# One wide product for the last queries of two heads, and a clamp and a rounding that change engines

## The chip, the core and the metric

The kernel runs on one core of a Trainium2 chip. The metric is the device time of one execution in microseconds (us). Of the core's engines this text uses short names: PE is TensorE (products; PEld its weight loads, which are rows of their own), DVE is VectorE, ACT is ScalarE, POOL is GpSimd, SP is SyncE, which issues most DMAs. Each engine works through its own list of instructions in order, and waits at an instruction until the semaphores that it names have come.

## The reference

Three stages in float32: an attention with a block-causal mask, a feed-forward layer that takes the maximum of three products, and a layer of four experts whose outputs are summed with weights.

```python
# attention: q, k, v of shape (4, 8, 576, 64)
scores = np.matmul(q, k.transpose(0, 1, 3, 2)) / np.sqrt(64)
scores = np.where(block_i >= block_j, scores, -1000000000.0)   # blocks of 64 positions
attn = softmax(scores)                                         # with + 1e-09 below the line
x = np.matmul(attn, v).transpose(0, 2, 1, 3).reshape(2304, 512)
# first layer: w1, w2, w3 (512, 768), w_out (768, 512)
x = np.maximum(np.maximum(x @ w1, x @ w2), x @ w3) @ w_out
# experts: w1 (4, 512, 1024), w2 (4, 1024, 512), p = domain_probs / (row sum + 1e-09)
out = sum(p[:, e:e + 1] * (np.maximum(x @ w1[e], 0) @ w2[e]) for e in range(4))
```

## The kernel before

**Numbers in two words.** A product in full float32 takes several passes on PE. Most products here are made from two rounded words instead: a number x is split into a high word (x rounded to the type float32r) and a low word (x minus the high word), and a product of two such numbers takes the products high by high, high by low and low by high. The heads of the first batch (`g < H`, eight of 32) use plain float32 in attention; the other 24 use split words.

**Attention.** The heads are walked in pairs. A pair's heads share one tile of queries: the last 64 of each head's 576 queries stand together in the tile `p4`, 128 rows, 64 of one head and 64 of the other. `scores` (lines 225 to 284) makes the scores of a tile of queries, takes the row extremes on DVE, the exponentials on ACT with their row sums, and lets POOL divide the rows by the sums (line 282). `turn_probs` (line 299) turns the tiles by PE transposes into a PSUM tile `tt`, from where ACT copies the high word `eh` (line 319) and DVE subtracts to get the low word `el` (line 320). Part 2 of it is the shared tile of last queries, turned once per pair: its columns are key block by key block, and within a block first the 64 queries of one head, then the 64 of the other.

`values` (line 357) makes the product with v for a split head. The stationary operand `vs[:, h, j]` holds the high word of v in columns 0 to 63 and the low word in 64 to 127, for one block j of keys, so that one product gives both in the upper and lower 64 rows of the result `pv`. What streams past is `eh` and then, in products of its own, `el`; both are summed into the same columns of PSUM. For the shared tile `products` (line 324) takes the head's 64 columns of each of the five key blocks, five products of 64 columns with `eh` and five with `el`, into columns 384 to 447. In the end ACT copies the other 64 rows to `tmp` (line 385) and DVE adds them to the head's own (line 386), which gives the head's part of `xf`, the transposed x of the pair. `moe1_inputs` (line 519) splits `xf` into `xh` (ACT, line 528) and `xl` (DVE, line 529) when a batch's heads are through.

**First layer.** `moe1` makes the first layer for one batch. Its products (`m`, line 510, 288 columns) are mixed by a planner into the attention of the next batch: `Filler` takes so many units after each step of a head, ten units behind. For the first batch the weights come from `Convert`, for the other three from a copy in HBM that it wrote. ACT and DVE evict the products (lines 546 and 548), POOL splits the hidden values (lines 550 and 551).

**Conversion.** The weights of the first layer are read as raw words of 64 bits, two words of 32 each, in 26 pieces, 18 of 512 columns and 8 of 384, and put together again as float32 values. `first` takes the magnitude of the upper word (ACT, line 433) and the scaled lower word (ACT, line 435). `second` clamps the magnitude (line 440), shifts it (442), joins it with the sign (443), and adds the lower word (POOL, 447). `third` rounds it to the high word (line 456, by the helper at line 82) and subtracts for the low word (457). `tick` runs these three as a pipeline, one or two pieces apart. The magnitudes have two buffers, the lower words one.

```python
nc.vector.tensor_scalar(a, a, MOST, LEAST, op0=ALU.min, op1=ALU.max)   # L440, the clamp
rounded(nc.gpsimd, high, a)                                            # L456, the rounding (runs at L82)
```

**Experts.** The last stage (lines 645 to 915) is products with split words throughout.

**Order.** The program is scheduled when it is built: a scheduler with a model of the engines' times puts the instructions of the first two stages into order on each engine. A small edit can so move many instructions against each other.

## Time and profile before

| | us |
|---|---|
| median of three runs | 1324.93 (1322.38 to 1325.15) |
| profiled execution, its own time | 1325.09 |
| its span, first to last instruction | 1323.4 |
| PE busy, PEld busy | 1286.8, 1185.8 |
| DVE, ACT, POOL busy | 917.8, 541.2, 629.9 |
| mean granted TensorE clock | 0.991 |

A busy time is a union: weight loads overlap each other and the products, and products overlap too, so a product's own length (say 256 ns) is not the time that it adds. That is read from the start of one load to the start of the next. A group's row ends with the idle time of its engine just before it and what ended it. The order rows below have no times: they show how the instructions stand in an engine's list, and in brackets the engines (with a number that says nothing here) whose semaphores an instruction waits for.

### The profile page before, as it was taken

The page shows a single profiled execution, that of the slowest core. Times are in us where ns is not written, and L with a number is a line of the kernel's source. Part 1 is how long each engine was busy: PE and PEld are TensorE (multiplying, and loading weights), DVE is VectorE, ACT ScalarE, POOL GpSimd, SP SyncE. Part 2 cuts the span into 40 slices and gives each one's busy share as a digit, 9 for nine tenths or more (in the row PEclk, how much of TensorE's full clock was granted, in tenths as well). Part 3 has the DMA queues.
Part 4 walks back from the last instruction along what each step waited for, and adds up shares of the span by engine and source line. Part 5 has one row for each costly group of instructions (what it writes and reads, how often), then busy time and mean ns, then how long its engine had stood idle before and what let it go on. Part 6 is the DMA issues. An engine that isn't in the chain of part 4 may idle for free.

```text
span 1323.4 us, 20932 instructions
## 1 busy us (share of the span) xinstructions
PE 1286.8 (97%) x7670; PEld 1185.8 (90%) x7670; DVE 917.8 (69%) x1685; ACT 541.2 (41%) x1219; POOL 629.9 (48%) x639
## 2 busy tenths in 40 slices
PE   7899999999999999999999999999999999999998
PEld 5669889999999989988999998999999899999997
DVE  6878999555656562178767788777777876777753
ACT  5676666444544430143333343333333433333331
POOL 4965776333334342165444455444444644454420
PEclk9899999999999999999999999999999999999999
DMA  8746677555444355232222223222222133222211
GB/s 204 216 122 167 200 224 204 162 156 133 141 123 116 112 176 161 79 96 64 76 69 64 64 64 95 81 64 64 74 79 72 55 110 91 64 64 64 64 33 48
DMA packets 146982, 142.85 MB, mean 108 GB/s; under 512 B 64576, under 2 KB 112704, under 8 KB 146880
## 3 DMA queue, kind: packets, MB, share of 16 engines
q1 hardware_dynamic: 144480, 132.18, 34.0%
q10 hardware_dynamic: 2400, 9.34, 3.1%
q8 instruction: 60, 0.98, 0.3%
q14 instruction: 42, 0.34, 0.1%
HBM read 114.86 MB, written 17.30 MB: 100 GB/s over the span
## 4 chain that ended last, share of the span: by engine, by line
PE 79%; DVE 8%; issue 3%; DMA 3%; POOL 3%; ACT 2%; SPq 0%; ACTq 0%; POOLq 0%; DVEq 0%
PE m L796 24%; PE m L510 17%; PE o L861 10%; PE o L859 10%; PE o L860 10%; PE st L250 3%; PE pv L374 2%; PE tt L314 2%; DMA q<-q 1%; PE pv L345 1%; POOL p L282 1%; ACT p L271 1%; DVE arena L443 1%; DVE t L718 1%; DMA pr<-in_moe_domain_probs 1%
## 5 line engine op out<-in xcount | busy, mean ns | idle before, releaser
L510 PE MATMUL m<-xh,wt 128*128 128x288 f32 x1152 | 258.0, 302 | 6.5 <-DVE mt L548 5.5
L859 PE MATMUL o<-w2h,hh 128*128 128x512 f32 x576 | 225.4, 392 | 4.9 <-DVE arena L866 4.9
L861 PE MATMUL o<-w2h,hl 128*128 128x512 f32 x576 | 225.5, 392 | 1.3 <-DVE hl L824 1.3
L860 PE MATMUL o<-w2l,hh 128*128 128x512 f32 x576 | 225.2, 391 | 0.0
L510 PEld LDWEIGHTS m<-xh,wt 128*128 128x128 f32 x1152 | 191.4, 188 | 9.1 <-DVE mt L548 5.3
L824 DVE SCALAR_TENSOR_TENSOR hl<-c,hh 128x384 fp32r<-128x384 f32 x144 | 168.3, 1189 | 37.4 <-ACT hh L823 37.1
L689 POOL TENSOR_TENSOR w2l<-r,w2h 128x512 fp32r<-128x512 f32 x96 | 130.1, 1375 | 89.8 <-ACT w2h L688 89.8
L510 PE MATMUL m<-xl,wt 128*128 128x288 f32 x576 | 170.2, 295 | 0.0
L689 POOL TENSOR_TENSOR sl<-s,sh 128x1024 fp32r<-128x1024 f32 x48 | 116.6, 2429 | 77.5 <-ACT sh L688 77.5
L689 POOL TENSOR_TENSOR al<-r,ah 128x512 fp32r<-128x512 f32 x48 | 64.7, 1348 | 180.6 <-ACT ah L688 177.2
L866 DVE SCALAR_TENSOR_TENSOR arena<-o,pr,arena 128x512 f32<-128x512 f32 x126 | 93.6, 743 | 71.5 <-PE o L861 71.4
L859 PEld LDWEIGHTS o<-w2h,hh 128*128 128x128 f32 x576 | 108.6, 189 | 24.0 <-DVE arena L866 6.0
L861 PEld LDWEIGHTS o<-w2h,hl 128*128 128x128 f32 x576 | 108.5, 188 | 22.5 <-DVE hl L824 1.7
L823 ACT ACTIVATE hh<-c 128x384 fp32r<-128x384 f32 x144 | 71.0, 519 | 135.9 <-DVE c L818 135.9
L860 PEld LDWEIGHTS o<-w2l,hh 128*128 128x128 f32 x576 | 108.6, 189 | 17.8
L282 POOL TENSOR_SCALAR p<-p,sm 128x128 f32<-128x128 f32 (+2 forms) x144 | 89.4, 640 | 58.7 <-DVE sm L280 27.9
L510 PEld LDWEIGHTS m<-xl,wt 128*128 128x128 f32 x576 | 108.4, 188 | 0.7
L271 ACT ACTIVATE p<-st,mn 128x128 f32<-128x128 f32 (+3 forms) x144 | 78.7, 553 | 51.1 <-DVE mn L264 50.9
L688 ACT CAST ah<-r 128x512 fp32r<-128x512 f32 x48 | 29.8, 620 | 156.3 <-issue 124.2
L548 DVE TENSOR_TENSOR mt<-m,mt 128x288 f32<-128x288 f32 x96 | 43.5, 454 | 63.8 <-PE m L510 61.5
L510 PE MATMUL m<-hh,wo 128*128 128x288 f32 x384 | 84.5, 301 | 0.4 <-ACT arena L559 0.4
L688 ACT CAST w2h<-r 128x512 fp32r<-128x512 f32 x96 | 59.1, 619 | 44.3 <-PE o L861 35.0
(166 smaller groups left out, 3000.1 us busy)
## 6 DMA issues: line engine op xcount, KB each, us to landing
wt<-held SPq DMA_DIRECT2D x54, 512.0 KB, 4.0
r<-in_moe_w SPq DMA_DIRECT2D x48, 512.0 KB, 3.9
r<-in_moe_w SPq DMA_DIRECT2D x96, 256.0 KB, 2.7
arena<-in_moe_w SPq DMA_DIRECT2D x18, 512.0 KB, 4.5
held<-wt SPq DMA_DIRECT2D x18, 512.0 KB, 3.4
wo<-held SPq DMA_DIRECT2D x12, 768.0 KB, 4.3
q<-q ACTq DMA_DIRECT2D x26, 304.0 KB, 4.5
arena<-in_q SPq DMA_DIRECT2D x32, 144.0 KB, 3.3
```

The lines of the kernel that those rows point to most:

```text
L271: nc.scalar.activation(x, st[:, o:o + w], ACTF.Exp, bias=mn[:, col:col + 1], scale=-1.0, accum_out=sm[:, col:col + 1],)
L282: nc.gpsimd.tensor_scalar(x, x, sm[:, col:col + 1], 1.0, op0=ALU.mult, op1=ALU.mult)
L510: nc.tensor.matmul(out=out_, lhsT=w, rhs=x, start=m == 0, stop=m == n - 1)
L688: nc.scalar.copy(dst_h, raw)
L689: (low or nc.gpsimd).tensor_tensor(dst_l, raw, f(dst_h), op=ALU.subtract)
L796: ins = nc.tensor.matmul(out=m, lhsT=w, rhs=x, start=start and n == 0, stop=stop and n == 3 * KH - 1, skip_group_check=True,)
L823: nc.scalar.activation(h, src, ACTF.Relu)
L824: nc.vector.scalar_tensor_tensor(l, src, 0.0, f(h), op0=ALU.max, op1=ALU.subtract)
L859: nc.tensor.matmul(out=o, lhsT=hh[:, ts], rhs=wh, start=i == 0, stop=False)
L860: nc.tensor.matmul(out=o, lhsT=hh[:, ts], rhs=wl, start=False, stop=False)
L861: nc.tensor.matmul(out=o, lhsT=hl[:, ts], rhs=wh, start=False, stop=i == G - 1)
L866: nc.vector.scalar_tensor_tensor(acc, ov, pr[:, tt, e:e + 1], acc, op0=ALU.mult, op1=ALU.add)
```

## The change

Two things are put together.

The shared tile gets one tile `e4` for both words, laid out as key block, head, word, query. For one head and one key block, the 64 columns of the high word and the 64 of the low word now lie side by side, and one product of 128 columns takes both. Its result fills columns 384 to 511 of `pv`: high-word products in 384 to 447, low-word products in 448 to 511. They are no longer summed in PSUM, so the copy to `tmp` takes 512 columns, DVE adds the last 64 columns into a new tile `last` (after's line 408), and once per pair POOL adds `last` to the last 64 columns of `xf` (after's line 410). Heads of the first batch use the high word of `e4` alone, in products of 64 columns as before.

In the conversion the clamp goes from DVE to POOL (after's line 462), and the rounding from POOL to ACT (it runs at line 80 of the helper).

```diff
--- before.py
+++ after.py
@@ -300,10 +300,15 @@
 
         hd = heads[g]
         banks = PARTS[part]
-        w = (1024, 256, 640)[part]
-        eh = ap_.tile([P, w], F32 if g < H else F32R, name="eh", tag=f"eh{part}", bufs=1)
-        el = None if g < H else ap_.tile([P, w], F32R, name="el", tag=f"el{part}", bufs=1)
-        (pairs[g // 2] if part == 2 else hd)["e", part] = (eh, el)
+        if part == 2:
+
+            e4 = ap_.tile([P, 5, 2, 2, 64], F32R, name="e4", tag="e4", bufs=1)
+            pairs[g // 2]["e4"] = e4
+        else:
+            w = (1024, 256)[part]
+            eh = ap_.tile([P, w], F32 if g < H else F32R, name="eh", tag=f"eh{part}", bufs=1)
+            el = None if g < H else ap_.tile([P, w], F32R, name="el", tag=f"el{part}", bufs=1)
+            hd["e", part] = (eh, el)
         pt = hd["p"] + [pairs[g // 2]["p4"]]
         for n in banks:
             o = 512 * (n - banks[0])
@@ -313,6 +318,16 @@
                 k0 = S - P if j == 4 else j * P
                 nc.tensor.transpose(tt[:, c:c + P], pt[i][:, k0:k0 + P], ident)
                 c += P
+            if part == 2:
+                j0, j1 = BANKS[n][0][0], BANKS[n][-1][0] + 1
+                high, low = (e4[:, j0:j1, :, x] for x in range(2))
+                src = tt[:, 0:c].rearrange("x (j h q) -> x j h q", h=2, q=64)
+                if g < H:
+                    nc.scalar.copy(f(high), src)
+                    continue
+                nc.scalar.copy(high, src)
+                nc.vector.tensor_tensor(low, src, f(high), op=ALU.subtract)
+                continue
             if g < H:
                 (nc.scalar.copy if n else nc.vector.tensor_copy)(eh[:, o:o + c], tt[:, 0:c])
                 continue
@@ -321,15 +336,12 @@
         if part == 1 and g % 2 == 0:
             turn_probs(g, 2)
 
-    def products(g, part):
-
-        h = g % 2
+    def products(part):
+
         todo = []
         for j in KEYS[part]:
             q0 = max(P, P * j)
-            todo.append((j, slice(q0 - P, 384), part, slice(BASE[j] + q0 - 512 * 2 * part, BASE[j] + 512 - 512 * 2 * part)))
-        if part:
-            todo += [(j, slice(384, 448), 2, slice(j * P + h * 64, j * P + h * 64 + 64)) for j in range(5)]
+            todo.append((j, slice(q0 - P, 384), slice(BASE[j] + q0 - 512 * 2 * part, BASE[j] + 512 - 512 * 2 * part)))
         return todo
 
     def values32(g, part):
@@ -339,11 +351,15 @@
             hd["pv"] = [ps_v.tile([P, 512], F32, name=f"pv{i}", tag="v") for i in range(2)]
             et = hd["e", 0][0]
             nc.tensor.matmul(out=hd["pv"][0][lo, 0:P], lhsT=vraw[:, h, 0], rhs=et[:, 0:P], start=True, stop=True)
-        for n, (j, to, which, of) in enumerate(products(g, part)):
-            et = (pairs[g // 2] if which == 2 else hd)["e", which][0]
-            rows = hi if j == 4 else both
+        et = hd["e", part][0]
+        todo = [(j, both, to, et[:, of]) for j, to, of in products(part)]
+        if part:
+            for j in range(5):
+                rows = hi if j == 4 else both
+                todo.append((j, rows, slice(384, 448), f(pairs[g // 2]["e4"][rows, j, h, 0])))
+        for n, (j, rows, to, x) in enumerate(todo):
             nc.tensor.matmul(
-                out=hd["pv"][1][lo, to], lhsT=vraw[rows, h, j], rhs=et[rows, of],
+                out=hd["pv"][1][lo, to], lhsT=vraw[rows, h, j], rhs=x,
                 start=part == 0 and n == 0, stop=j == 4,
             )
         if part == 0 and h == 0:
@@ -367,25 +383,31 @@
                     out=hd["pv"][0][:, 0:P], lhsT=vs[:, h, 0], rhs=et[:, 0:P], start=n == 0, stop=n == 1
                 )
         pv = hd["pv"][1]
-        todo = products(g, part)
-        for n in range(2):
-            for m, (j, to, which, of) in enumerate(todo):
-                et = (pairs[g // 2] if which == 2 else hd)["e", which][n]
-                nc.tensor.matmul(
-                    out=pv[:, to], lhsT=vs[:, h, j], rhs=et[:, of],
-                    start=part == 0 and n == 0 and m == 0, stop=part == 1 and n == 1 and j == 4,
-                )
+        todo = [(j, to, et[:, of]) for et in hd["e", part] for j, to, of in products(part)]
+        if part:
+            todo += [(j, slice(384, 512), pairs[g // 2]["e4"][:, j, h]) for j in range(5)]
+        for n, (j, to, x) in enumerate(todo):
+            nc.tensor.matmul(out=pv[:, to], lhsT=vs[:, h, j], rhs=x, start=part == 0 and n == 0, stop=j == 4)
         if part == 0 and h == 0:
             pairs[g // 2]["xf"] = mp.tile([P, S], F32, name="xf", tag="xf", bufs=4)
         xf = pairs[g // 2]["xf"]
         own, other = (lo, hi) if h == 0 else (hi, lo)
         qs = (slice(0, P), slice(P, S))[part]
-        src = hd["pv"][part][:, 0:qs.stop - qs.start]
-        tmp = ap_.tile([P, S - P], F32, name="tmp", tag="tmp", bufs=1)[own, 0:qs.stop - qs.start]
+        w = qs.stop - qs.start
+        n = (P, 512)[part]
+        src = hd["pv"][part][:, 0:n]
+        tmp = ap_.tile([P, 512], F32, name="tmp", tag="tmp", bufs=1)[own, 0:n]
         nc.scalar.copy(tmp, src[other])
-        nc.vector.tensor_tensor(xf[own, qs], src[own], tmp, op=ALU.add)
+        nc.vector.tensor_tensor(xf[own, qs], src[own, 0:w], tmp[:, 0:w], op=ALU.add)
         if part == 0:
             return
+
+        if h == 0:
+            pairs[g // 2]["last"] = ap_.tile([P, 64], F32, name="last", tag="last", bufs=1)
+        last = pairs[g // 2]["last"]
+        nc.vector.tensor_tensor(last[own], src[own, w:n], tmp[:, w:n], op=ALU.add)
+        if h:
+            nc.gpsimd.tensor_tensor(xf[:, S - 64:S], xf[:, S - 64:S], last, op=ALU.add)
         del heads[g]
 
 
@@ -437,7 +459,7 @@
         def second(self, i):
             a = self.buf(i, "a")
             au, high = a.bitcast(U32), self.words(i)[1]
-            nc.vector.tensor_scalar(a, a, MOST, LEAST, op0=ALU.min, op1=ALU.max)
+            nc.gpsimd.tensor_scalar(a, a, MOST, LEAST, op0=ALU.min, op1=ALU.max)
 
             nc.vector.tensor_scalar(au, au, 3, None, op0=ALU.logical_shift_left)
             nc.vector.scalar_tensor_tensor(
@@ -453,7 +475,7 @@
                 tag, bufs = ("wt", WT) if n < 3 * NF else ("wo", 2)
                 self.made[n] = mp.tile([P, 2, tiles[n].shape[1], P], F32R, name=tag, tag=tag, bufs=bufs)
             high, low = (self.made[n][:, j, s].rearrange("p a f -> p (a f)") for j in range(2))
-            rounded(nc.gpsimd, high, a)
+            rounded(nc.scalar, high, a)
             nc.vector.tensor_tensor(low, a, f(high), op=ALU.subtract)
             nc.sync.dma_start(
                 out=held[n][:, :, s.start * P:s.stop * P],
```

On PE, the shared tile's products of the thirteenth split head (the results are `pv_4044` before and `pv_4001` after, the stationary operand is `vs`, what streams is `eh` and `el`; `m` is the first layer), before:

```order
L510 MATMUL m<-xh,wt 128x288
L374 MATMUL pv_4044<-eh,vs 128x256
L374 MATMUL pv_4044<-eh,vs 128x64 x5
L374 MATMUL pv_4044<-el,vs 128x256
L374 MATMUL pv_4044<-el,vs 128x64 x5
L510 MATMUL m<-xh,wt 128x288
```

and after:

```order
L532 MATMUL m<-xh,wt 128x288
L390 MATMUL pv_4001<-eh,vs 128x256
L390 MATMUL pv_4001<-el,vs 128x256
L390 MATMUL pv_4001<-e_3972,vs 128x128 x5
L532 MATMUL m<-xh,wt 128x288
```

Ten products of 64 columns have become five of 128, behind the 256-column products of the third key block, and nothing else stands between.

On DVE, the conversion beside the fifth split head (`arena` holds a piece's words, `wt` the finished weights; line 440 is the clamp, 442 the shift, 443 the joining, 457 the low word), before:

```order
L320 TENSOR_TENSOR el<-tt,eh 128x128 [waits Activation_49]
L440 TENSOR_SCALAR arena<-arena 128x512 [waits Activation_49]
L457 TENSOR_TENSOR wt<-arena,wt 128x512 [waits DMAHW2_49,Pool_49]
L442 TENSOR_SCALAR arena<-arena 128x512 [waits DVE_49]
L386 TENSOR_TENSOR xf<-pv_2156,tmp 64x128 [waits Activation_49]
L443 SCALAR_TENSOR_TENSOR arena<-arena 128x512 [waits DMAHW7_49,DVE_49]
L440 TENSOR_SCALAR arena<-arena 128x512 [waits Activation_49]
```

and after, where the shift is line 464, the joining 465, the low word 479:

```order
L401 TENSOR_TENSOR xf<-pv_2141,tmp 64x128 [waits Activation_49]
L479 TENSOR_TENSOR wt<-arena,wt 128x512 [waits DMAHW3_49,Activation_49,Pool_49]
L570 TENSOR_TENSOR mt<-m,mt 128x288 [waits DVE_49,PE_49]
L464 TENSOR_SCALAR arena<-arena 128x512 [waits Pool_49]
L465 SCALAR_TENSOR_TENSOR arena<-arena 128x512 [waits DMAHW1_49,DVE_49]
L260 MEMSET st 64x64 [waits PE_49]
L401 TENSOR_TENSOR xf<-pv_2142,tmp 64x448 [waits Activation_49]
L408 TENSOR_TENSOR last<-pv_2142,tmp 64x64
```

The clamp is gone, the shift waits for POOL, where it waited for DVE alone, and the small add into `last` is new.

On POOL, behind the split of v (`vs`) of a later pair (line 447 is the integer add, 82 the rounding, 550 and 551 the split of hidden values), before:

```order
L167 TENSOR_TENSOR vs<-vraw,vs 128x2x4x64
L167 TENSOR_TENSOR vs<-vraw,vs 64x2x64 [waits Pool_49]
L447 TENSOR_TENSOR arena<-arena 128x512 [waits DVE_49,Activation_49,Pool_49]
L82 TENSOR_SCALAR wt<-arena 128x512 [waits DMAHW0_49,PE_49,Pool_49]
L447 TENSOR_TENSOR arena<-arena 128x512 [waits DVE_49,Activation_49]
L82 TENSOR_SCALAR wt<-arena 128x512 [waits DMAHW2_49,PE_49,Pool_49]
L447 TENSOR_TENSOR arena<-arena 128x512 [waits DVE_49,Activation_49]
```

and after, where the clamp is line 462 and the integer add 469:

```order
L167 TENSOR_TENSOR vs<-vraw,vs 128x2x4x64
L167 TENSOR_TENSOR vs<-vraw,vs 64x2x64 [waits Pool_49]
L469 TENSOR_TENSOR arena<-arena 128x512 [waits DVE_49,Activation_49,Pool_49]
L462 TENSOR_SCALAR arena<-arena 128x512 [waits Activation_49]
L572 TENSOR_SCALAR hh<-mt 128x288 [waits DVE_49]
L462 TENSOR_SCALAR arena<-arena 128x512 [waits Activation_49]
L573 TENSOR_TENSOR hl<-mt,hh 128x288 [waits Pool_49]
L469 TENSOR_TENSOR arena<-arena 128x512 [waits DVE_49]
```

The clamp stands in POOL's list where the rounding stood; the rounding's wait for PE is no longer there, and the clamp waits for ACT.

On ACT, between the evictions of the fifth split head's turned tiles (`eh`, in after `e` for the shared tile; lines 433 and 435 take a piece's upper and lower word), before:

```order
L319 CAST eh<-tt 128x256 [waits PE_49]
L435 ACTIVATE arena<-arena 128x512 [waits Pool_49]
L319 CAST eh<-tt 128x512 [waits PE_49]
L319 CAST eh<-tt 128x128 [waits PE_49]
L433 ACTIVATE arena<-arena 128x512 [waits DMAHW7_49,DVE_49]
L435 ACTIVATE arena<-arena 128x512 [waits Pool_49]
```

and after (455 and 457):

```order
L334 CAST eh<-tt 128x256 [waits PE_49]
L457 ACTIVATE arena<-arena 128x512 [waits Pool_49]
L80 CAST wt<-arena 128x512
L328 CAST e_2097<-tt 128x8x64 [waits PE_49]
L328 CAST e_2097<-tt 128x2x64 [waits PE_49]
L455 ACTIVATE arena<-arena 128x512 [waits DMAHW1_49,DVE_49]
```

The rounding (line 80) stands right behind the instruction that waits for POOL, and has no wait of its own there.

## Rows read from the trace of the kernel before

**Rows 1.** The page, its first line and section 1.

```profile
span 1323.4 us, 20932 instructions
...
PE 1286.8 (97%) x7670; PEld 1185.8 (90%) x7670; DVE 917.8 (69%) x1685; ACT 541.2 (41%) x1219; POOL 629.9 (48%) x639
```

**Rows 2.** Busy time by stretch, columns in the first line.

```profile
core 0: us, PE busy (x) PEld busy (x) DVE busy (x) ACT busy (x) POOL busy (x), PEclk, DMA share, GB/s
...
30.00:60.00 30.00, 24.52 (x133) 19.16 (x132) 24.63 (x53) 21.33 (x60) 23.80 (x29) 0.80 0.75 202
...
100.00:130.00 30.00, 30.00 (x231) 29.35 (x230) 25.77 (x67) 20.56 (x52) 15.01 (x22) 1.00 0.57 150
130.00:160.00 30.00, 27.44 (x204) 26.32 (x204) 28.62 (x66) 17.10 (x44) 23.86 (x32) 1.00 0.64 206
160.00:190.00 30.00, 27.73 (x202) 26.04 (x201) 28.91 (x74) 19.73 (x51) 22.27 (x28) 1.00 0.66 206
190.00:235.00 45.00, 44.37 (x336) 43.02 (x335) 41.84 (x97) 26.86 (x70) 30.46 (x45) 1.00 0.77 221
235.00:475.00 240.00, 238.94 (x1840) 237.27 (x1839) 137.65 (x381) 111.19 (x304) 84.03 (x147) 1.00 0.47 134
...
545.00:1323.00 778.00, 765.64 (x3877) 693.79 (x3875) 553.05 (x776) 268.23 (x498) 359.29 (x243) 0.99 0.24 72
```

**Rows 3.** Weight loads in order of time: start us, length us, line.

```profile
327.65 0.19 PEld L366 LDWEIGHTS pv<-eh,vs 128*128 128x128 f32 x1
327.78 0.19 PEld L366 LDWEIGHTS pv<-el,vs 128*128 128x128 f32 x1
327.89 0.19 PEld L250 LDWEIGHTS st<-kk,q 128*128 128x128 f32 x1
...
330.54 0.77 PEld L374 LDWEIGHTS pv<-eh,vs 128*128 128x128 f32 x6
331.23 0.76 PEld L374 LDWEIGHTS pv<-el,vs 128*128 128x128 f32 x6
331.90 0.19 PEld L510 LDWEIGHTS m<-xh,wt 128*128 128x128 f32 x1
```

**Rows 4.** Groups by form, whole span (count, busy us, mean ns, idle).

```profile
L374 PE MATMUL pv<-eh,vs 128*128 128x64 f32 x120 | 16.1, 256 | 0.0
```

**Rows 5.** The same group, 235 to 475 us.

```profile
L374 PE MATMUL pv<-eh,vs 128*128 128x64 f32 x80 | 10.8, 255 | 0.0
```

**Rows 6.** Groups by form, conversion and evictions, 0 to 545 us.

```profile
L447 POOL TENSOR_TENSOR arena<-arena 128x512 int32<-128x512 int32 x18 | 24.1, 1337 | 9.4 <-DVE arena L443 7.2 <-ACT tmp L385 2.0
...
L385 ACT COPY tmp<-pv 64x448 f32<-64x448 f32 x24 | 12.7, 528 | 40.0 <-PE pv L374 38.2 <-PE tt L314 1.6
...
L82 POOL TENSOR_SCALAR wt<-arena 128x512 fp32r<-128x512 f32 x18 | 12.0, 668 | 8.5 <-PE m L510 7.8
...
L167 POOL TENSOR_TENSOR vs<-vraw,vs 64x128 fp32r<-64x128 f32 x12 | 6.9, 573 | 0.9
L386 DVE TENSOR_TENSOR xf<-pv,tmp 64x128 f32<-64x128 f32 x24 | 6.9, 286 | 2.2 <-ACT tmp L385 1.9
...
L82 POOL TENSOR_SCALAR wo<-arena 128x384 fp32r<-128x384 f32 x8 | 4.9, 617 | 0.3
...
L688 ACT CAST ah<-r 128x512 fp32r<-128x512 f32 x2 | 1.2, 623 | 0.0
```

**Rows 7.** Busy time of line 440 alone, by stretch (us, count).

```profile
30.00:100.00 70.00, 4.13 (x7) 0.90 0.63 170
100.00:235.00 135.00, 8.55 (x19) 1.00 0.67 198
```

**Rows 8.** Waits, 100 to 235 us: total us, times, longest us.

```profile
POOL arena L447 <- DVE arena L443: 10.9, 7, 3.8
...
POOL wt L82 <- PE m L510: 7.8, 3, 6.0
...
PE m L510 <- DVE mt L548: 3.5, 4, 1.4
```

## The prediction

> **What bounds the kernel now.** The page first [rows 1]: TensorE (PE) is busy 97% of a span of 1323.4 us, its weight loads (PEld) 90%. Then the busy time by stretch [rows 2]. Three regimes matter. From 235 to 475 us, where attention and the first feed-forward layer share PE, weight loads are busy 237.27 of 240 us: PE is the bound, every other engine has a third or more to spare. From 100 to 235 us, where the first layer's weights are also converted, PE falls to 129.5 of 135 us and VectorE (DVE) stands at 125.1 of 135, over 95% from 130 to 190: the two are nearly equal bounds. From 30 to 60 us no engine is full (DVE 24.6, POOL, that is GpSimd, 23.8 of 30 us). The 778 us from 545 on are the second layer. The instruction order there is the same in both kernels, so I take it as unchanged.
>
> Then the weight loads in order of time, since PE's busy time hides its pace [rows 3]. A load is 0.19 us long, but loads overlap: the group of six that starts at 331.23 (one product of 256 columns, five of 64) is followed by the next load at 331.90, so 0.67 us for six, 0.112 us each. A product of 128 columns (327.78) is followed by the next load after 0.11 us too. A product of 64 columns therefore costs as much PE time as one of 128.
>
> **The products.** Each of 24 heads issues ten 64-column products of the shared tile (120 with eh [rows 4], and as many with el). Now it issues five of 128 columns. Removed: 120 loads with their products, at 0.112 us, 13.4 us of PE. The remaining 120 double their columns at no cost if 0.11 us holds. At most they cost the longer step of a 128-column product in these rows, 0.13 us (327.65 to 327.78): per head 10 x 0.112 - 5 x 0.13 = 0.47 us, 11 us for 24. Between 11 and 13.4 us I take 13.4, since two of three rows agree on 0.11. By time: 80 of the 120 lie after 235 us [rows 5], 9.0 us, on an engine that waits for nothing there, so they come off the end. 40 lie between 100 and 235 us, 4.5 us of PE.
>
> The Trainium skill, page "TensorE: Matmul & The Clock Gate", section "Back-to-back issue gap", gives about 60 cycles for 1 to 64 columns and 134 for 128, so by it ten narrow ones and five wide ones would cost nearly the same. This trace disagrees: 0.112 us at 64 columns, 0.11 at 128 [rows 3]. I keep it as a rival below.
>
> **What the products add.** The ScalarE (ACT) copy of the head's result grows from 448 to 512 columns: at 528 ns for 448 [rows 6], at most 64/448 of it, 0.08 us, 24 times, beside an ACT that is under two thirds busy. DVE gets a 64x64 add per head, bounded by nothing and the 286 ns of the 64x128 add [rows 6]; I take 0.25 us, 6 us in all, 2 us of it in the stretch where DVE is full. POOL gets 12 adds of 128x64, bounded by nothing and 573 ns [rows 6], about 6 us, 2 of them before 235 us. Each POOL add stands between the result and the split of x for the feed-forward layer. Only at a batch's last pair does that split follow at once (three times); the previous batch's products still fill PE then, so I count nothing. Without that cover it would be some 0.25 + 0.57 us each, 2.5 us in all. The strided copies into the shared tile have the sizes of the copies that they replace: nothing.
>
> **The conversion.** There are 26 pieces, 18 of 512 columns and 8 of 384. DVE loses its clamps: 4.13 us before 100 us, 8.55 between 100 and 235 [rows 7]. POOL loses 26 roundings (12.0 + 4.9 us) and gets 26 clamps. No clamp on POOL is shown. The nearest row is the rounding itself, also one input and two constants, 668 ns [rows 6]; the other end is the two-input add of the same shape, 1337 ns. I take 668: POOL's load stays as it is. At the other end it grows by 17 us. ACT gets 26 roundings at 623 ns or less [rows 6], 16 us, some 12 of them between 100 and 235 us, where it has 84 of 135 us busy. They are queued in front of exponentials and evictions that PE needs; but in most places of the order each stands right behind an instruction that already waits for POOL's add, so it brings its length and hardly a wait. What POOL waited for before, PE giving a weight buffer free (7.8 us in three waits [rows 8]), now falls on ACT.
>
> The new coupling is the clamp's: DVE's shift of a piece now waits for POOL, and what is queued behind it on DVE (maxima, evictions of the feed-forward products, for which PE waited 3.5 us [rows 8]) waits with it. Before, DVE waited for ACT alone there. POOL in turn waits at its integer add for DVE, as before (10.9 us [rows 8]).
>
> The Trainium skill, page "GPSIMD Engine Reference", section "Engine selection", says to put an elementwise maximum on VectorE, since POOL is about two times slower with two inputs, near line rate with one. The clamp has one input, and POOL's rounding at 668 ns against 1337 for two inputs [rows 6] fits; if the clamp ran at the two-input rate, the slow rival below would follow.
>
> Net for 100 to 235 us: PE loses 4.5 us of work, DVE 8.55 - 2 = 6.5. Both bounds fall by about 5%, so the stretch falls by at least PE's 4.5; the 5.5 us that PE stands idle there (135 - 129.5) are the most that DVE's relief can add. I take 1 us of these, as DVE's load falls only a little faster than PE's: 5.5 us. For 30 to 100 us: DVE 4.1 us less, ACT about 4 more, POOL even: 0.5 us.
>
> **The sum**, against the profiled execution's own 1325.09 us (the span and 1.7 us around it; the median shown is 1324.93, the same within 0.2 us): 1325.1 - 9.0 - 5.5 - 0.5 = 1310.1 us.
>
> **Rivals.** (a) The conversion exchange pays in full: all 5.5 us of PE's idle time and 2 us before 100 us. 1325.1 - 9.0 - 10 - 2 = 1304. For it: DVE over 95% busy where PE idles. Against: the clamp now passes one engine more. (b) The stretch before 235 us gains nothing, because POOL or ACT takes DVE's place as the engine waited for: only 9.0 us, 1316. For it: five handovers per piece instead of three. (c) The change doesn't do what it says: PE's pace goes by columns, so that five products of 128 cost what ten of 64 did. Then 0.11 is the wide one's step, the narrow ones take half of it, and the products give nothing. With 1 us from the conversion, 1324. Against: the six loads in 0.67 us [rows 3] are mostly narrow ones. This is where the rule of the Trainium skill quoted above would end.
>
> (d) Slower: DVE stalls at the shift behind POOL's clamp. Place: 26 shifts in DVE's queue between 30 and 235 us. If each holds DVE for w us, the stretch before 235 us changes by 26w - 12.7 (the clamps gone) + 2 (the adds), and with the 9.0 us behind it the total is slower by over 2.7 us once w passes about 0.86 us. A clamp of 1.34 us with POOL busy in front of it would do that. At w = 1.2 it is 31.2 - 10.7 - 9.0 = 11.5 us: 1337. For it: POOL at 77% from 130 to 190 us, standing in order behind its own waits for DVE. Against: the order puts other work on DVE between, and the 668 ns.
>
> **How the numbers follow.** Forecast (1306 to 1314) 0.53; (a) 0.15; (b) 0.17; (c) 0.06; (d) 0.09. Predicted is the likeliest, 1310. The range of 1302 to 1321 takes in (a), (b) and the bound of 11 us on the products; it leaves out (c), (d) and a little below (a). What the measurement can tell from no change is 0.2%, 2.7 us: faster 0.53 + 0.15 + 0.17 = 0.85, the same 0.06 from (c), slower 0.09 from (d).
>
> **What would show it.** In the changed profile: 7550 products instead of 7670; 128-column products of the shared tile followed by the next load after 0.11 us (0.13 or more speaks for (c)); POOL's clamp near 0.67 us; ACT's roundings near 0.62; the second layer's stretch again 778 us; the end of the conversion some 5 us earlier. DVE waiting for POOL's clamp by more than some 10 us in total would be (d); ACT held at its rounding by PE for several us would be (b). The forecast is wrong if the conversion's stretch grows, or if the stretch behind it doesn't shrink by about 9 us.

## The result and the profile after

The changed kernel takes 1303.76 us (median of 4 runs, 1302.49 to 1305.25). The kernel before took 1324.48 us in the same series (1322.38 to 1325.15). The ratio is 0.984, with a 95% interval of 0.9827 to 0.9853: 20.7 us less, where 15 were forecast. The sign and the range held, and 1303.76 is nearly the time of rival (a). But part of the sum came out in other places than the forecast had put it, and how much of it the conversion is worth depends on the order of the instructions.

The profiled execution took 1305.25 us, 1.7 us of it around the span. Its first line and section 1, as in [rows 1]:

```profile
span 1303.5 us, 20731 instructions
...
PE 1272.5 (98%) x7550; PEld 1174.2 (90%) x7550; DVE 903.5 (69%) x1683; ACT 554.1 (43%) x1245; POOL 632.7 (49%) x651
```

There are 120 products fewer. ACT is 12.9 us busier and DVE 14.3 us less busy. POOL is even (632.7 against 629.9), as forecast. Busy time by stretch, with the columns of [rows 2]:

```profile
30.00:60.00 30.00, 29.30 (x175) 21.65 (x175) 24.30 (x58) 24.70 (x68) 25.16 (x34) 0.89 0.75 196
60.00:100.00 40.00, 37.59 (x236) 27.42 (x235) 28.69 (x74) 27.96 (x78) 25.96 (x35) 0.96 0.62 165
100.00:130.00 30.00, 29.87 (x230) 29.55 (x229) 25.67 (x66) 21.24 (x54) 18.17 (x27) 1.00 0.52 155
130.00:160.00 30.00, 30.00 (x233) 29.82 (x232) 27.64 (x72) 22.03 (x55) 23.56 (x33) 1.00 0.69 204
160.00:190.00 30.00, 29.33 (x223) 28.69 (x223) 27.66 (x74) 21.77 (x55) 24.32 (x34) 1.00 0.70 208
190.00:235.00 45.00, 41.92 (x291) 40.59 (x290) 40.99 (x103) 33.90 (x88) 28.97 (x41) 0.92 0.72 223
235.00:475.00 240.00, 235.85 (x1799) 233.86 (x1798) 143.93 (x388) 114.34 (x301) 96.04 (x155) 1.00 0.51 145
```

From 130 to 190 us PE now stands idle 0.7 us; before it was 4.8 [rows 2]. From 190 to 235 us it is idle 3.1 us at a granted clock of 0.92, where it was idle 0.6 at 1.00: a new wait, which is followed up below. Since the kernel now runs ahead, equal times no longer hold equal work, so the ledger goes by marks: the last split of x (the instruction that makes xh) of batches 1 to 4, in the profiled executions, in us. The last two columns count the first-layer products (`m`) that PE starts in each stretch.

```
                        before   after   difference   products before   after
start to batch 1         101.5    97.4      -4.1                    4       4
to batch 2               127.7   116.4     -11.3                  530     489
to batch 3               124.7   127.4      +2.7                  557     614
to batch 4               120.8   114.3      -6.5                  582     570
to the end               848.8   848.0      -0.8
```

The forecast had -0.5 us for the first row, -5.5 up to 235 us (the mark of batch 2 lies at 229.2 us before) and -9.0 behind it. Up to that mark the change brought 15.4 us, behind it 4.5. A part of this is work that moved: 41 first-layer products fewer stand before the mark and 57 more right behind it. At about 0.13 us each (an estimate, from the two load steps from 316.65 to 316.90 us shown below) they are 5.3 and 7.4 us. With the same work the three stretches between the marks would be 6.0, 4.7 and 4.9 us shorter, and 40 removed products take about 4.4 us in each.

From the first product of the experts' layer (at 562.5 us before, 543.7 after) to the end it is 760.8 us before and 759.7 after: unchanged, as forecast.

The products' step can be read as in [rows 3]. These are weight loads of the changed kernel in order of time (start us, length us, engine, line); the group of seven from 315.84 is one head's:

```profile
315.70 0.19 PEld L532 LDWEIGHTS m<-xh,wt 128*128 128x128 f32 x1
315.84 0.19 PEld L390 LDWEIGHTS pv<-eh,vs 128*128 128x128 f32 x1
315.97 0.19 PEld L390 LDWEIGHTS pv<-el,vs 128*128 128x128 f32 x1
316.08 0.64 PEld L390 LDWEIGHTS pv<-e,vs 128*128 128x128 f32 x5
316.65 0.19 PEld L532 LDWEIGHTS m<-xh,wt 128*128 128x128 f32 x1
316.76 0.19 PEld L532 LDWEIGHTS m<-xl,wt 128*128 128x128 f32 x1
316.90 0.32 PEld L532 LDWEIGHTS m<-xh,wt 128*128 128x128 f32 x2
```

Five 128-column products take 316.08 to 316.65, 0.114 us each. The head's group takes 0.81 us from its first load to the next one's; before it took 1.36 (330.54 to 331.90 [rows 3]). The difference, 0.55 us, is the price of five products at 0.11, and 24 heads give 13.2 us, if all are like this one.

The conversion's moved instructions, and the products' new ones, by form (count, busy us, mean ns, idle before them and what ended it):

```profile
L400 ACT COPY tmp<-pv 64x512 f32<-64x512 f32 x24 | 13.9, 581 | 32.9 <-PE pv L390 28.7 <-PE tq L195 2.5 <-DVE xf L401 1.4
L462 POOL TENSOR_SCALAR arena<-arena 128x512 f32<-128x512 f32 x18 | 12.1, 673 | 16.8 <-ACT arena L455 15.8
L80 ACT CAST wt<-arena 128x512 fp32r<-128x512 f32 x18 | 11.3, 630 | 0.8 <-PE m L532 0.8
L410 POOL TENSOR_TENSOR xf<-xf,last 128x64 f32<-128x64 f32 x12 | 5.6, 464 | 11.3 <-DVE last L408 10.8
L408 DVE TENSOR_TENSOR last<-pv,tmp 64x64 f32<-64x64 f32 x24 | 5.1, 213 | 0.0
```

The clamp takes 673 ns on POOL (668 was taken), the rounding 630 ns on ACT (623). ACT is held at its rounding by PE for only 0.8 us.

### The profile page after: what moved, and what is told of

It reads as the page before. It is cut to its first block, busy times and chain, and to the rows that moved or that the text cites. A ratio compares the mean times of both kernels' runs of the same rounds, so it can differ in the third digit from the quotient of the medians.

```text
span 1303.5 us, 20731 instructions
## 1 busy us (share of the span) xinstructions
PE 1272.5 (98%) x7550; PEld 1174.2 (90%) x7550; DVE 903.5 (69%) x1683; ACT 554.1 (43%) x1245; POOL 632.7 (49%) x651
## 4 chain that ended last, share of the span: by engine, by line
PE 86%; DVE 5%; DMA 3%; POOL 2%; ACT 2%; issue 2%; SPq 0%; ACTq 0%; POOLq 0%; DVEq 0%
PE m L818 24%; PE m L532 21%; PE o L883 10%; PE o L881 10%; PE o L882 10%; PE st L250 4%; PE pv L390 3%; PE tt L319 3%; PE pv L361 1%; DMA vraw<-in_v 1%; DMA wo<-held 1%; ACT p L271 1%; PE tq L195 1%; DVE t L740 1%; PE tq L176 1%
## 5 line engine op out<-in xcount | busy, mean ns | idle before, releaser
L532 PE MATMUL m<-xh,wt 128*128 128x288 f32 x1152 | 253.2, 300 | 2.8 <-DVE mt L570 2.0
L282 POOL TENSOR_SCALAR p<-p,sm 128x128 f32<-128x128 f32 (+2 forms) x144 | 85.4, 611 | 52.7 <-DVE sm L280 34.1
```

The costliest lines, as they stand in the source:

```text
L282: nc.gpsimd.tensor_scalar(x, x, sm[:, col:col + 1], 1.0, op0=ALU.mult, op1=ALU.mult)
L532: nc.tensor.matmul(out=out_, lhsT=w, rhs=x, start=m == 0, stop=m == n - 1)
```

## The experiments

The theory was the forecast's: the products pay 0.112 us each, most of it behind 235 us, and the conversion little, through DVE's load. The rivals were that the conversion pays, or that the gain before 235 us is luck of the order. All ratios are to the kernel before in the same series, with 95% intervals.

### One part of the change at a time

e1: the wide products, conversion as before.

```
-            nc.gpsimd.tensor_scalar(a, a, MOST, LEAST, op0=ALU.min, op1=ALU.max)
+            nc.vector.tensor_scalar(a, a, MOST, LEAST, op0=ALU.min, op1=ALU.max)
...
-            rounded(nc.scalar, high, a)
+            rounded(nc.gpsimd, high, a)
```

> The wide products with the conversion as before (clamp on DVE, rounding on POOL). Theory A (each of 120 removed products is worth one step of 0.112 us, and PE is the bound wherever they stood): 13.4 us less than before, about 1311. Theory B (the 40 products before 235 us give nothing while DVE is full there; only the conversion's edits free that stretch): 9 us less, about 1315.5, and the stretch up to the end of the conversion as long as before. Theory C (the order that the scheduler makes decides): anything, with PE stalls at new places and the granted clock low behind them.

e2: the same two lines changed in the kernel before, products as before.

> The clamp on POOL and the rounding on ACT, products as before. Theory A (the two edits add up): the rest of the 20.7 us, so 7 us less than before, about 1317. Theory B (the edits need each other): 3 us less or nothing, 1321 to 1324. Theory C (order): no fixed size; the gain or loss sits in a few PE stalls and the low clock behind them.

e3: the changed kernel with the rounding back on POOL (the second pair of lines alone).

> The changed kernel with the rounding back on POOL: DVE is relieved of 12.7 us, POOL gets 17 us more, ACT nothing. If DVE's load is what counted: 1304 to 1307, as fast as the whole change. If POOL is then waited for (rival d of the prediction in a milder form): 1311 or more, with DVE idle before the shift for POOL's clamp.

e4: the changed kernel with the clamp back on DVE (the first pair alone).

> The changed kernel with the clamp back on DVE: POOL is relieved of 17 us, ACT gets 16 more, DVE is as loaded as before. If DVE's load is what counted: about 1311, as with the products alone. If POOL's load was what counted: about 1304. If the rounding on ACT is what makes PE wait (2.3 us for it at 202 us in the changed profile), this kernel has that wait too, and the products alone or with the clamp alone don't.

```
                                us (median)   ratio [95%]
before                             1325.28
e1 products alone                  1314.07    0.9917 [0.9903, 0.9930]
e2 conversion alone                1311.30    0.9898 [0.9884, 0.9912]
e3 products and clamp              1322.21    0.9974 [0.9964, 0.9985]
e4 products and rounding           1317.44    0.9943 [0.9931, 0.9955]
```

Measured, the conversion alone is worth 14.0 us in this order, more than either size written down for it; the products alone are worth 11.2. In the kernel with wide products, moving the clamp alone costs 8.1 us (e3 against e1), moving the rounding alone costs 3.4 (e4 against e1), and moving both gains 10.3 (1303.76 against e1). The last compares two series, whose kernels before differ by under 1 us. The 3.4 us of e4 are no more than a mere change of order makes (below).

By the marks, e1 reaches batch 2 at 229.8 us, where the kernel before is at 229.2: the 40 products taken out before that mark bring nothing there, and the 11 us come off behind it, which is its theory B. e2 is the opposite: 4.5 us come off before the first mark, 9.1 up to batch 2 (12 fewer first-layer products are 1.6 of them), and 1.5 are given back behind it.

PE's idle time from 100 to 235 us goes with the times of e1, e2 and e3, but not with that of e4, where PE is as idle as in e1. The one row of each kernel, with the columns of [rows 2], first e1, then e2, e3 and e4:

```profile
100.00:235.00 135.00, 127.22 (x937) 121.60 (x935) 125.75 (x309) 86.19 (x215) 97.23 (x128) 1.00 0.69 200
```

```profile
100.00:235.00 135.00, 134.23 (x1030) 132.57 (x1029) 121.42 (x304) 99.13 (x255) 92.72 (x129) 1.00 0.68 205
```

```profile
100.00:235.00 135.00, 123.92 (x911) 119.60 (x911) 119.54 (x313) 89.38 (x232) 97.60 (x147) 0.99 0.64 184
```

```profile
100.00:235.00 135.00, 127.23 (x956) 123.66 (x957) 123.40 (x307) 95.64 (x237) 81.84 (x109) 1.00 0.69 201
```

PE is idle 7.8, 0.8, 11.1 and 7.8 us; in the kernel before it was 5.5 [rows 2]. e3 relieves DVE most and has the most idle PE: POOL then clamps, adds and rounds every piece, the last piece is ready at 260.6 us (229.6 in e1), and PE waits for the pieces. These are PE's waits in e3 (us in total, times, longest):

```profile
PE m L532 <- DVE wo L479: 3.5, 1, 3.5
PE st L250 <- DMA q<-q: 2.5, 2, 1.3
PE tt L319 <- DVE kk L211: 2.0, 3, 1.3
PE m L532 <- DVE wt L479: 1.0, 1, 1.0
```

In e2 the 3.5 us for which PE waited on DVE's evictions [rows 8] are gone, and PE's waits in that stretch come to 0.7 us:

```profile
PE tt L314 <- DVE kk L211: 0.5, 1, 0.5
PE st L250 <- DVE el L320: 0.2, 1, 0.2
```

### The products undone inside the change

e5: the changed kernel, the wide tile read by ten 64-column products per head.

```
-            todo += [(j, slice(384, 512), pairs[g // 2]["e4"][:, j, h]) for j in range(5)]
+            todo += [(j, slice(384 + 64 * x, 448 + 64 * x), pairs[g // 2]["e4"][:, j, h, x]) for x in range(2) for j in range(5)]
...
-            nc.tensor.matmul(out=pv[:, to], lhsT=vs[:, h, j], rhs=x, start=part == 0 and n == 0, stop=j == 4)
+            nc.tensor.matmul(out=pv[:, to], lhsT=vs[:, h, j], rhs=x, start=part == 0 and n == 0, stop=n == len(todo) - 1 and part == 1)
```

> The changed kernel with the shared tile read as ten products of 64 columns again, one per key block and word, each word into its own columns; copies, adds and conversion as in the changed kernel. If the number of products is what the wide form saves (a step of 0.112 us each): 120 x 0.112 = 13.4 us more than the changed kernel where PE is the bound, so 1313 to 1317, and 9 us of it between the end of the conversion and the end of attention. If PE's pace goes by columns (rival c): the same as the changed kernel, 1304.

Measured: 1312.88 us, 0.9906 [0.9889, 0.9922], so the wide products are worth 8.7 us here (0.9906 less 0.9840, of 1324.5) and 11.2 us in e1, not the whole 13.2. The stretch to batch 4 takes 120.5 to 121.4 us with narrow products (before, e2, e5) and 114.3 or 114.4 with wide ones (after, e1, e4). Of these 6 us, 40 products make 4.5. The rest is mostly that 12 first-layer products now fall into other stretches (570 instead of 582); at about 0.13 us each, estimated as above, that is 1.6 us. The changed kernel with another order (e8, below) takes 121.1 us there: 625 first-layer products fall into it.

### DVE's load taken away

f1: the kernel before with the clamp's line left out.

```
-            nc.vector.tensor_scalar(a, a, MOST, LEAST, op0=ALU.min, op1=ALU.max)
```

> The kernel before without the clamp at all (this part of the computation is left out), everything else as before: DVE is relieved of 12.7 us, POOL and ACT are as loaded as before, and a piece has no more handovers than before. If DVE's load is what the stretch up to 235 us goes by: about 1311, as with both conversion edits alone. If the conversion edits alone gained by something else (fewer waits of POOL for free weight buffers, an order that happens to be better): 1318 to 1324.

Measured: 1325.11 us, 0.9997 [0.9987, 1.0008]. DVE loses the clamps that it loses in the change (its busy time falls by 9.7 us, from 917.8 to 908.1) and no engine gets them, yet the time stays. PE's idle time from 100 to 235 us falls from 5.5 to 3.1 us, and its wait for DVE's evictions from 3.5 us [rows 8] to 1.0:

```profile
100.00:235.00 135.00, 131.94 (x992) 128.49 (x991) 119.37 (x286) 86.08 (x219) 94.87 (x130) 0.99 0.70 202
```

```profile
PE tq L195 <- ACT p L271: 1.8, 1, 1.8
PE m L509 <- DVE mt L547: 1.0, 2, 0.6
```

The stretch from batch 1 to batch 2 is 3.9 us shorter (123.8 against 127.7), about 2 of which are 15 first-layer products that move behind it. But the first mark comes 2.9 us later (104.4 us against 101.5), and the later stretches give back another 2.2. So a lighter DVE does let PE stand less in that stretch, by 2 to 4 us, but in this order the time gains nothing from it, and it is not enough for the 14.0 us of e2.

### How much is luck of the order

LAG is the number of first-layer steps by which the written order keeps that layer behind the attention; it is 10. f2 and e7 set it to 14 and 9 in the kernel before, e11 and e8 in the changed one.

> The kernel before with the first layer's products four units further behind attention; work, engines and buffers are the same. It says how far the order alone moves the kernel before. If the order matters little there: 1322 to 1328. If it matters as in the changed kernel (1304 to 1310 for the same edit): a difference of 5 us or more either way, and PE waits and low clock at other places.

> The kernel before with the first layer's products one unit closer to attention; a second such change of the order alone. If the order matters little: 1322 to 1328. If the order of the kernel before is an unlucky one (its clock is at half for 6.8 us twice before 65 us): 1315 to 1320.

> The changed kernel with the first layer's products four units further behind attention. Work, engines and buffers are the same, only the order differs. If PE came to the conversion's last pieces too early: 1297 to 1301, with no wait for a piece of the output weights. If the order alone moves the time by several us either way (theory C), it lands anywhere from 1300 to 1310 with its PE waits elsewhere.

> The changed kernel with the first layer's products one unit closer to attention; the order alone differs. If the wait of 2.3 us at 202 us and the 6.8 us at half clock behind it belong to this one order: 1299 to 1303. If the conversion's chain is late in any order: 1303 to 1308.

```
LAG    before                             after                              gain
 9     1321.49  0.9969 [0.9952, 0.9985]   1308.66  0.9874 [0.9859, 0.9889]   12.8
10     1324.48                            1303.76  0.9840 [0.9827, 0.9853]   20.7
14     1327.32  1.0019 [1.0009, 1.0028]   1309.79  0.9883 [0.9861, 0.9905]   17.5
```

A step that changes no arithmetic moves either kernel by 2 to 6 us. The change gains in all three orders, by 12.8 to 20.7 us; the forecast's 15 lies between, and the order in use has the largest gain. If the products' 13.2 us of PE come off in each of them, the rest of the change gives 7.5 us at LAG 10, 4.3 at 14 and -0.4 at 9 (an estimate). With the 11.2 or 8.7 us that e1 and e5 measured in their place, each is 2.0 or 4.5 us more, and the three still lie 8 us apart. So what the conversion's moves are worth goes by the order. They were not run alone at another LAG.

### The new wait at 202 us

In the changed kernel PE stands 2.26 us for one ACT rounding. ACT's instructions before it (start, length, engine, line, and in brackets its idle time):

```profile
200.72 0.74 ACT L581 COPY arena<-m 128x288 f32<-128x288 f32 x2
201.99 0.37 ACT L334 CAST eh<-tt 128x256 fp32r<-128x256 f32 x1 [0.52 <-PE tt L319]
202.42 1.20 ACT L208 ACTIVATE q<-tq 64x512 fp32r<-64x512 f32 x2
203.64 0.55 ACT L457 ACTIVATE arena<-arena 128x384 int32<-128x384 uint32 x1
204.10 0.49 ACT L80 CAST wo<-arena 128x384 fp32r<-128x384 f32 x1
```

The piece's add had ended on POOL at 201.7 us; its rounding began at 204.10, behind three other lines of ACT's queue (201.99 to 204.10). Windows of 5 us of the changed kernel, with the columns of [rows 2]:

```profile
200.00:205.00 5.00, 2.57 (x16) 2.19 (x17) 4.83 (x19) 4.35 (x12) 4.81 (x9) 1.00 0.55 200
205.00:210.00 5.00, 4.89 (x25) 4.70 (x24) 4.77 (x12) 4.11 (x13) 3.92 (x8) 0.57 0.78 217
210.00:215.00 5.00, 5.00 (x31) 5.00 (x30) 3.89 (x9) 2.77 (x6) 4.59 (x8) 0.75 0.92 267
215.00:220.00 5.00, 5.00 (x43) 5.00 (x42) 4.64 (x8) 4.29 (x10) 1.98 (x3) 1.00 0.69 200
```

PE is idle 2.4 us, and then the granted clock is 0.57 and 0.75: for part of these 10 us it is at 1.2 GHz instead of 2.4. That is 5 x 0.43 + 5 x 0.25 = 3.4 us of PE's pace, so the wait costs 5.8 us at most. That the whole kernel grows by the 3.4 us isn't shown. In the 45 runs of the kernel before that were made beside the experiments the mean granted clock goes from 0.991 to 0.997, and the time doesn't go with it: the six at 0.991 average 1325.3 us and the four at 0.996 1325.5, though 0.005 of 1323 us are 6.6 us. Two tries to remove it: e6 rounds the last eight pieces (those of wo) on POOL again, e9 lets the conversion run two pieces further ahead.

```
-            rounded(nc.scalar, high, a)
+            rounded(nc.scalar if n < 3 * NF else nc.gpsimd, high, a)
```

> The changed kernel with the rounding of the last eight pieces (those of the output weights) back on POOL; the other 18 stay on ACT. If ACT's queue is what made PE wait 2.3 us for such a piece at 202 us (its add ended 2.4 us before its rounding began), the wait and the low clock behind it go: 1298 to 1302. If the conversion's chain as a whole is late there, the wait moves to another instruction of the piece: 1303 to 1306.

```
-            self.upto(sum(i <= n for i, _ in pieces))
+            self.upto(sum(i <= n for i, _ in pieces) + 2)
```

> The changed kernel with the conversion run two pieces further ahead of the weights' first use in the program. If the conversion's chain paces the stretch up to its end at 229 us (PE waits for it at 202 us): it ends some 5 to 10 us earlier, and the time is 1297 to 1301. If the magnitudes' two buffers and DVE's load pace it, the end stays near 229 us and the time near 1304.

Measured: e6 1307.73 us, 0.9871 [0.9851, 0.9891]; e9 1304.28 us, 0.9841 [0.9824, 0.9859]. In e6 PE waits 1.6 us at 200.7 for a DVE subtraction instead, and the clock falls all the same (200 to 205 us: 0.69, 205 to 210: 0.63). In e9 the same wait stands, 2.26 us, and the conversion ends at 228.5 us instead of 228.8, so running it ahead hardly made it earlier. In e11 the wait is gone and the clock stays at 1.00 from 200 to 215 us, but other waits take its place (1.6 us before a pair's transposes at 202, 1.6 us on the DMA of q at 214.6). In e8 such a wait comes at 232 us, of 1.2 us. e2 and e4 round on ACT too and have no such wait, so the rounding on ACT alone doesn't make it. None of the versions beat the changed kernel: e6 missed both of the ranges written down for it, and e11 and e8 came out slower than the changed kernel though the wait at 202 us is gone.

## Why the prediction was right, and where it was not

**The products: right in price.** The step of a 64- and of a 128-column product is the same, 0.11 us, and 24 heads save 13.2 us of PE (13.4 forecast). Rival (c) is refuted: here five wide products take 0.57 us and six mostly narrow ones 0.67 [rows 3]. The table of the Trainium skill (page "TensorE: Matmul & The Clock Gate", section "Back-to-back issue gap") that gives 64 columns about half the cycles of 128 is meant there for the gap of a product by itself, and the forecast read it too far. Of a stream in which each product has its weight load the same section says that both set the spacing, and it gives about 81 ns at 128 columns; this trace has a load before each product and 114 ns.

Wrong in place: not all of it shows if nothing else changes. In e1 the "4.5 us of PE" before 235 us don't come off at all by the mark of batch 2 (229.8 us against 229.2). Between the first two marks PE is idle 7.8 us instead of 4.9 and makes 6 first-layer products more (0.8 us), which is most of the 4.5: without the conversion's change PE arrives earlier and waits longer. In the whole change the stretch behind the mark of batch 2 shrinks by 4.5 us, where the forecast called itself wrong if it "doesn't shrink by about 9 us". That is the 57 first-layer products that moved there; at equal work it is 4.7 + 4.9 = 9.6 us (an estimate).

**The conversion: too small in this order, and the reason is not borne out.** The forecast said of DVE and PE that "the two are nearly equal bounds", let DVE's relief act on PE's 5.5 idle us, and took "1 us of these, as DVE's load falls only a little faster than PE's", and 0.5 us before 100 us. The term of 1.5 us measured 14.0 in e2. f1 takes the same clamps off DVE and the time stays, so DVE's load alone doesn't make the difference, though PE stands 2.4 us less in that stretch. With the clamp on POOL and the rounding on ACT, 4.7 of the 5.5 us go (e2: 0.8 left). With only one of the two moved, PE is idle more than before (e3, e4). That these are waits behind single instructions in a queue, which go or come with the place of each step, fits the waits shown, but why just this pair does it was not settled. What is shown is that e3 puts three steps of each piece on POOL and ends the conversion 31 us later than e1. A part is order: at LAG 9 what is left for all but the products is -0.4 us, or 1.6 to 4.1 with the figures of e1 and e5 (estimates), and the forecast's 1.5 would be near it.

**The first stretch: the "0.5 us" was 4.** In the kernel before PE waits 1.79 us from 54.0 us on for a DVE copy, and the granted clock falls behind it. The product after the wait, and the windows:

```profile
55.83 0.90 PE L176 MATMUL tq<-idents,spare 128*128 128x128 f32 x3 [1.79 <-DVE spare L185]
```

```profile
50.00:55.00 5.00, 4.04 (x30) 2.85 (x27) 4.98 (x10) 4.84 (x14) 4.76 (x6) 0.99 0.63 206
55.00:60.00 5.00, 4.17 (x20) 4.17 (x20) 4.83 (x11) 3.57 (x12) 3.58 (x6) 0.50 0.92 229
60.00:65.00 5.00, 5.00 (x22) 2.62 (x22) 4.91 (x15) 3.12 (x9) 4.83 (x7) 0.82 0.86 267
```

The same windows of the changed kernel:

```profile
50.00:55.00 5.00, 5.00 (x36) 4.06 (x36) 2.87 (x8) 4.66 (x14) 4.76 (x7) 1.00 0.96 260
55.00:60.00 5.00, 5.00 (x37) 3.68 (x36) 3.93 (x11) 3.75 (x11) 3.68 (x8) 1.00 0.61 124
60.00:65.00 5.00, 5.00 (x27) 2.89 (x26) 4.81 (x13) 2.97 (x9) 4.73 (x6) 1.00 0.87 262
```

The clock is only a part of it. From 60 to 100 us the kernel before has

```profile
60.00:100.00 40.00, 39.42 (x244) 26.82 (x244) 28.95 (x81) 27.83 (x80) 28.33 (x39) 0.98 0.55 146
```

and the changed kernel 0.96 (above). So from 30 to 100 us PE loses 30 x 0.20 + 40 x 0.02 = 6.8 us of its pace before and 30 x 0.11 + 40 x 0.04 = 4.9 after, 1.9 less, and up to 100 us it is idle 11.2 us instead of 14.1.

The wait goes with the clamp's place. The six kernels with the clamp on DVE or with none (before, e1, e4, f1, f2, e7) have a wait of PE of 1.2 to 1.8 us between 50 and 56 us (in five of them for this copy, in e4 for ACT), and reach the first mark at 99.3 to 104.4 us. The eight with the clamp on POOL have none there over 0.6 us, but for e3 (1.2 us at 57.8, for a DMA), and reach it at 95.3 to 99.0. f1 has the wait without any clamp on DVE, so the clamp's load isn't what makes it; what does was not settled. The clock falls behind the wait in five of the six, in f1 it stays at 1.00 from 48 to 65 us. That a slow clock can follow a short wait was in the windows of before [rows 2: 0.80 from 30 to 60 us], and the forecast did not price it.

**The rivals.** (a) came closest to the time, but its reason, "DVE over 95% busy where PE idles", is not borne out: in f1 the same relief leaves the time where it was. (b)'s sign, ACT held at its rounding by PE, stayed at 0.8 us; but PE held by ACT's rounding came instead, at 202 us. (d) didn't come: DVE waited for POOL's clamp 0.5 us at its shift and 0.8 at a low word, at a clamp of 0.67 us. The end of the conversion was forecast some 5 us earlier and came 3.8 us earlier (232.6 to 228.8). PE reached the first product with the output weights some 14 us earlier (208.4 to 194.1), so it now catches up with the conversion there: that is the wait at 202 us.

**The sum, put together from the marks:** 4.1 us before the first mark; 6.0, 4.7 and 4.9 in the next three stretches, with the moved first-layer products counted at their price; 0.8 behind: 20.5, where the spans differ by 19.9. Of these, 13.2 are the products' price, in three parts of 4.4. Some 7 us are left for all else, 4.1 of them before the first mark. The experiments don't add up as neatly: e1's span fell by 11.1 us and e2's by 12.1, 23.2 together, and the 5.8 us at most of the new wait would explain the 3.3 too many, but no run without that wait is faster. The profiled execution is also only one: the clock's mean in it is 0.990, and in the three others, 0.994, the spans are 1300.7 to 1302.5 us. That the total came out near the forecast is in part luck: the conversion was counted at 1.5 us and gave 14.0 alone in this order, the products before 235 us give nothing without it, and the same change gains 12.8 us at LAG 9.

## What to carry to other kernels

Read PE's pace from load start to load start, and price a removed product at that step. An engine that is 95% busy is a bound only when taking work off it moves the time; otherwise look for the single waits, and at whether the clock falls behind them. Compare equal work: a stretch between two marks can be shorter because work has moved out of it. Where an order is written out, reshuffle it once without changing the work: here that moved either kernel by 2 to 6 us, so a single term of that size can't be believed from one order.

## What the runs showed of the hardware that was not expected

A wait of PE of about 2 us was at times followed by half clock: 3.4 us of PE's pace lost in the 10 us behind the 2.26 us wait at 202 us, and 5 x 0.50 + 5 x 0.18 = 3.4 us behind the 1.79 us wait at 54.0. At times it was not: behind the 1.6 us wait at 202 us in e11 and a wait of 2.2 us at 204 us in e8 the clock stays at 1.00 up to 215 us. And a run's mean granted clock did not tell its time: 45 runs of the kernel before, from 0.991 to 0.997, show no trend (1325.3 us on average at 0.991, 1325.5 at 0.996).

With the wide products, the clamp alone on POOL cost 8.1 us, and clamp and rounding moved together gained 10.3 in the order in use; the rounding alone on ACT cost 3.4, no more than a change of order does.
